# Eleven unread matrix products among the transposes of w2 and around the first scores

## The chip, the cores and the metric

The kernel runs on one core of a Trainium2 chip. The metric is the device time of one execution in microseconds. Of a kernel timed several times the median is given; one execution is profiled, and its span (first to last instruction) is a little shorter than its time.

## The reference

Four inputs q, k, v and f_logit have the shape batch 4, heads 8, sequence 768, head width 48. A gated linear recurrence runs over the sequence, and its output goes through a maxout layer.

```python
f = 1 / (1 + exp(-f_logit))
state = f[t][:, None] * state + outer(k[t], v[t])      # per batch and head, 48 x 48
y[t] = q[t] @ state
x = y as 3072 tokens x 384
out = maximum(x @ w1, x @ w2) @ w_out                   # w1, w2: 384 x 1024, w_out: 1024 x 384
```

## The kernel before

The sequence is cut into chunks of 128 positions; with four batches that makes 24 tiles, numbered i, each of all 8 heads. The first four tiles are the first chunks of the four batches, which have no earlier state.

For each tile, ACT computes exp and ln of the gate logits (`e`, `ln`), and TensorE sums the logs over the chunk with a triangular matrix (`cum`, L218). ACT turns the sums into factors `ei` and `ed`. DVE or GpSimd scales k and q with them (`kp`, `qp`, with `kpv`, `qpv` for those on DVE), TensorE transposes both (`trk`, `trq`, or `tr` for both at once, L263), and DVE copies the transposes out of PSUM (`trke`, `trqe`, `tre`). TensorE forms the scores of all heads (`a`, L281), DVE multiplies them with the causal mask (`am`, L286), and TensorE applies them to v (`y`, L326). ACT copies the result to `x`, TensorE transposes it (`xT`, L336).

The maxout is rewritten: max(h1, h2) is h2 plus the positive part of h1 - h2. So the kernel needs wd = w1 - w2 (`wd` on DVE, `wdp` on GpSimd) and w2o = w2 @ w_out. For w2o the prologue casts w2 to bf16 (`w2c` on DVE, `w2ca` on ACT), transposes it in eight blocks f of three 128 x 128 pieces (`w2T`, L186), copies each block out (`w2Te`, L189 on DVE), casts w_out (`woc`, L176 on ACT) and multiplies (`w2o`, L196). Each tile then takes x @ wd (`d0`, `d1`, L350), the positive part (`g0`, `g1`, on ACT) and x @ w2o + g @ w_out (`o0`, `o1`, L368), which DVE copies (`ob`) and a transfer stores.

The order of the instructions on every engine is written out by hand. The strings PROLOGUE, STEP and EPILOGUE list pairs of an operation's name and a number; `run` looks the name up in the table `ops` and issues it. Each engine, and SP's queue, which issues the loads, works through its own instructions in that order. PROLOGUE sets everything up to tile 6 or so, STEP repeats, EPILOGUE drains.

PSUM is divided into three pools: `ps_s` with three buffers (tag "s": cumulative sums, transposes, y, state products), `ps_a` with one buffer of two banks (tag "a": the scores), and `ps_m` with three buffers (tag "mm": transposed w2, w2o, d, o). The operation `warm n` takes one "mm" buffer and issues n products of 128 x 128 with 128 x 512 into it. Their inputs are the gate logs of tile 1, with zeros in the padding. Nothing reads their output; the buffer's next user overwrites it. The prologue has `warm 5`, `warm 3` and `warm 1`, nine products in all.

`run` drops an operation that was issued already, except `warm`.

Of the kernel before, what the change touches and what calls it, by code (L numbers as in the profile page):

```python
# [10 lines left out]
F32 = mybir.dt.float32  # L11
# [3 lines left out]


PROLOGUE = """
setup 0  setup 2  setup 1  lf 1  lf 0  lq 0  lw2 2  lk 0  lw2 0  lw2 1  lv 0  lwo 0  e 0
lwo 1  e 1  ln 1  lk 1  ln 0  cum 0  cum 1  lw1 0  w2ca 2  warm 5  ei 0  lw1 2  fl 0  ed 0
kp 0  ei 1  qpv 0  ed 1  fl 1  lw1 1  w2c 0  warm 3  warm 1  lq 1  w2ca 1  w2T 0  lf 2  w2T 7  # L20
trk 0  w2Te 7  trq 0  w2T 4  trke 0  w2Te 0  trqe 0  w2T 5  w2T 1  a 0  lv 1  am 0  w2Te 1
w2Te 4  v 0  lq 2  woc 2  w2T 2  y 0  w2Te 2  w2Te 5  woc 0  w2T 6  lk 2  w2T 3  woc 1  w2Te 6
w2o 2  kpv 1  w2o 1  x 0  w2Te 3  trk 1  lf 3  wdp 0  woc 3  xT 0  trke 1  w2o 5  xTe 0
w2o 4  w2o 7  w2o 10  lv 2  w2o 8  w2o 0  sa 0  wd 2  w2o 11  w2o 3  lk 3  w2oe 2  w2o 6
w2oe 1  w2o 9  wd 1  w2oe 0  lq 3  qpv 1  d1 0  lf 4  e 2  trq 1  d0 0  ln 2  trqe 1  tmp 0
lf 5  a 1  g0 0  v 1  cum 2  am 1  ed 2  lv 3  o0 0  g1 0  qp 2  ei 2  y 1  fl 2  lq 4  kpv 2
o1 0  x 1  xT 1  trk 2  xTe 1  lk 4  e 3  trq 2  trke 2  d0 1  ln 3  trqe 2  ob 0  lk 5
cum 3  a 2  v 2  ed 3  d1 1  g0 1  am 2  lv 4  ei 3  g1 1  o0 1  kpv 3  lq 5  y 2  qp 3
o1 1  x 2  fl 3  xT 2  lv 5  e 4  tr 3  xTe 2  ln 4  sa 1  d0 2  tre 3  lf 6  ob 1  cum 4
g0 2  a 3  d1 2  ed 4  lk 6  v 3  am 3  ei 4  g1 2  o0 2  lq 6  qp 4  e 5  tmp 1  y 3  fl 4  # L30
o1 2  x 3  st 0  lf 7  kpv 4  ln 5  xT 3  tr 4  xTe 3  sa 2  lk 7  cum 5  tre 4  d0 3  ob 2
a 4  lv 6  v 4  g0 3  d1 3  am 4  ei 5  ed 5  lv 7  g1 3  o0 3  qp 5  tmp 2  fl 5  y 4  kpv 5
lq 7  o1 3  x 4  st 2  xT 4  lq 9  e 6  tr 5  xTe 4  st 1  sa 3  ln 6  d0 4  tre 5  lf 8
ob 3  cum 6  g0 4  dq 4  a 5  v 5  d1 4  ed 6  am 5  lq 8  ei 6  qp 6  g1 4  o0 4  tmp 3  fl 6
out 2  e 7  y 5  kpv 6  o1 4  x 5  lk 8  ln 7  xT 5  tr 6  xTe 5  sa 4  lf 9  d0 5  tre 6
ob 4  cum 7  g0 5  dq 5  a 6  out 0  v 6  d1 5  ed 7  am 6  ei 7  lv 8  qp 7  g1 5  o0 5  tmp 4
y 6  kpv 7  out 1  o1 5  x 6  st 3  fl 7  xT 6  tr 7  lk 9  e 8  xTe 6  sa 5  ln 8  tre 7
lk 10  ob 5  v 7  lf 10
"""

STEP = """
# [23 lines left out]
def kernel(  # L65
# [13 lines left out]
    nc = tc.nc  # L79
    B, H, S, D = q.shape  # L80
    C = 128
# [6 lines left out]
    NP = H // 2  # L88
# [6 lines left out]
    ps_s = ctx.enter_context(tc.tile_pool(name="ps_s", bufs=3, space=bass.MemoryType.PSUM))  # L95
    ps_a = ctx.enter_context(tc.tile_pool(name="ps_a", bufs=1, space=bass.MemoryType.PSUM))
    ps_m = ctx.enter_context(tc.tile_pool(name="ps_m", bufs=3, space=bass.MemoryType.PSUM))
# [7 lines left out]
    ell_b = [consts.tile([C, H, DP], BF16, name=f"ell{n}") for n in range(2)]  # L105
# [10 lines left out]
    wd = consts.tile([C, JG, d_ff], BF16, name="wd")  # L116
    wo = consts.tile([C, FG, dm], BF16, name="wo")
    w2T = consts.tile([C, FG, dm], BF16, name="w2T")
    w2o = consts.tile([C, JG, dm], BF16, name="w2o")
# [23 lines left out]
    st = {}  # L143
# [209 lines left out]
    def a_g(i, half):  # L353
        s = st[i]
        if half == 0:
            s["g"] = work.tile([C, FG, C], BF16, name="gT", tag="gT", bufs=3)
        nc.scalar.activation(s["g"][:, half * 4:half * 4 + 4, :], psum.pop(("d", half, i)), AF.Relu)  # L357

    def p_o(i, half):
        s = st[i]  # L360
        if half == 0:
            psum["o", i] = ps_m.tile([C, dm], F32, name="o", tag="mm")
        mms = [(s["xT"][:, j, :], w2o[:, j, :]) for j in range(JG)]
        mms += [(lambda f=f: s["g"][:, f, :], wo[:, f, :]) for f in range(FG)]
        cut = 6
        for n in (range(0, cut) if half == 0 else range(cut, len(mms))):
            l, r = mms[n]
            nc.tensor.matmul(out=psum["o", i], lhsT=l() if callable(l) else l, rhs=r,  # L368
                             start=(n == 0), stop=(n == len(mms) - 1))
# [5 lines left out]
    def store(i, eng=nc.sync):  # L375
        c, b = divmod(i, B)
        r0 = b * S + c * C
        eng.dma_start(out=out[r0:r0 + C, :], in_=st[i]["ob"])
# [13 lines left out]
    def ob_last(h):  # L392
        t = st[T - 1]["ob", h] = consts.tile([C, dm // 2], F32, name=f"obl{h}")
        if h == 0:
            nc.scalar.copy(t, psum.pop(("last", h)))
        else:
            nc.vector.tensor_copy(t, psum.pop(("last", h)))
# [2 lines left out]
        r0 = B * S - C  # L400
        nc.sync.dma_start(out=out[r0:r0 + C, h * dm // 2:(h + 1) * dm // 2], in_=st[T - 1]["ob", h])

    def warm(n):

        ps = ps_m.tile([C, 512], F32, name="warm", tag="mm")
        for _ in range(n):
            nc.tensor.matmul(out=ps, lhsT=ell_b[1][:, 0:2, :].rearrange("p h d -> p (h d)"),
                             rhs=ell_b[1].rearrange("p h d -> p (h d)"), start=True, stop=True)

    ops = {  # L410
# [14 lines left out]
        "dq": lambda i: p_d(i, 1, True),  # L425
        "g0": lambda i: a_g(i, 0), "g1": lambda i: a_g(i, 1),
        "o0": lambda i: p_o(i, 0), "o1": lambda i: p_o(i, 1), "ob": v_ob, "out": store, "outa": lambda i: store(i, nc.scalar), "warm": warm,
        "lo": p_last, "lob0": lambda n: ob_last(0), "lob1": lambda n: ob_last(1),
        "lout": store_last,
    }  # L430
# [2 lines left out]
    done = set()  # L433

    def run(op, n):
        key = (same.get(op, op), n)
        if op == "warm" or key not in done:
            done.add(key)
            ops[op](n)

# [4 lines left out]
    for op, n in pairs(PROLOGUE):  # L445
        run(op, n)
    last = pairs(EPILOGUE)
    kept = split_up | {(same.get(op, op), n) for op, n in last}
    for i in range(FIRST_STEP, T + 8):
        for op, n in pairs(STEP):  # L450
            if 0 <= i + n < T and (same.get(op, op), i + n) not in kept:
                run(op, i + n)
    for op, n in last:
        run(op, n)
# [30 lines left out]
```

## Time and profile before

| what | value |
|---|---|
| time, median of 4 runs | 146.83 us (144.96 to 149.3) |
| time of the profiled execution | 144.96 us |
| its span | 143.2 us |
| mean granted TensorE clock | 0.988 |
| PE busy | 129.3 us, 90% of the span |
| PEld (weight loads) busy | 100.1 us, 70% |
| DVE busy | 106.5 us, 74% |
| ACT busy | 87.1 us, 61% |
| GpSimd (POOL) busy | 68.9 us, 48% |
| HBM traffic | 198 GB/s over the span |

In the profile, PE is TensorE's matrix products and PEld its weight loads, which overlap them; DVE is VectorE, ACT ScalarE, POOL GpSimd, and SP the engine that issues loads. A line such as L350 is a line of the kernel, and `out<-in` names the tiles written and read. The slices of the page cut the span into 40 equal parts; a digit is the busy share in tenths, and the clock row has the granted TensorE clock in tenths. The chain of waits is followed back from the last instruction to what released each step. Times stand in microseconds from the start of the span. An idle time before an instruction stands in brackets, with what ended it.

### The profile page before, as it was taken

What the parts mean: (1) busy time and instruction counts of PE and PEld (TensorE: products, weight loads), DVE (VectorE), ACT (ScalarE), POOL (GpSimd) and SP (SyncE); (2) the same over time, 40 slices, a digit from 0 to 9 for tenths busy, and PEclk for the clock granted to TensorE, in tenths of its full rate; (3) what the DMA queues carried; (4) which work ended last, traced back from release to release, by engine and by line L of the source; (5) the groups of instructions that cost most, each with busy time, mean ns of one, the idle gap of its engine ahead of it and who ended that gap; (6) DMA issues with size and microseconds to landing.
All of it is one profiled execution on the core that took longest, in us unless ns stands there. A gap on an engine that the chain in (4) does not pass through costs nothing.

```text
span 143.2 us, 4345 instructions
## 1 busy us (share of the span) xinstructions
PE 129.3 (90%) x1756; PEld 100.1 (70%) x1756; DVE 106.5 (74%) x191; ACT 87.1 (61%) x183; POOL 68.9 (48%) x98
## 2 busy tenths in 40 slices
PE   0096499999999999999999999999999999999981
PEld 0044357688778877887888788778878887887771
DVE  7825866796898789778977797798779777976521
ACT  3572454966677575758566765767585757663440
POOL 8520060220848485567657655855685546442000
PEclk9999959999999999999999999999999999999999
DMA  4999999999899997998999999999999999971111
GB/s 93 246 352 387 341 324 183 168 206 177 178 162 189 182 229 198 218 206 189 219 196 205 199 179 222 218 191 219 234 195 199 221 224 201 200 222 60 55 55 55
DMA packets 105764, 28.62 MB, mean 200 GB/s; under 512 B 101521, under 2 KB 104721, under 8 KB 105745
## 3 DMA queue, kind: packets, MB, share of 16 engines
q1 hardware_dynamic: 103728, 25.60, 85.6%
q10 hardware_dynamic: 2016, 2.75, 5.8%
q8 instruction: 13, 0.21, 0.6%
q14 instruction: 7, 0.05, 0.1%
HBM read 23.59 MB, written 4.72 MB: 198 GB/s over the span
## 4 chain that ended last, share of the span: by engine, by line
PE 85%; DMA 6%; SPq 5%; ACT 2%; issue 1%; DVE 1%
PE o L368 29%; PE d L350 25%; PE tr L263 7%; DMA wo_f<-in_moe_w_out_dram 6%; PE a L281 5%; PE w2op L196 4%; PE y L326 3%; PE xtp L336 3%; PE cum L218 3%; PE y L321 2%; PE sa L295 2%; SPq L152 2%; SPq L157 2%; SPq L161 1%; ACT wo L176 1%; PE o L389 1%
## 5 line engine op out<-in xcount | busy, mean ns | idle before, releaser
L350 PE MATMUL d<-xT,wd 128*128 128x128 bf16 x576 | 43.4, 220 | 0.5 <-DVE xT L340 0.4
L256 POOL TENSOR_TENSOR qp<-qt,ed 128x384 bf16<-128x384 f32 x22 | 22.1, 1003 | 44.4 <-ACT ed L230 30.5
L350 PEld LDWEIGHTS <-wd 128*128 128x128 bf16 x576 | 36.5, 114 | 4.3 <-issue 0.6
L368 PE MATMUL o<-wo,gT 128*128 128x384 bf16 x184 | 37.4, 325 | 0.0
L357 ACT ACTIVATE gT<-d 128x512 bf16<-128x512 f32 x48 | 28.9, 603 | 9.6 <-PE d L350 9.4
L286 DVE TENSOR_TENSOR am<-a,mask 128x1024 bf16<-128x1024 f32 x24 | 29.4, 1223 | 1.0 <-PE a L281 0.5
L340 DVE COPY xT<-xtp 128x384 bf16<-128x384 bf16 x24 | 8.6, 357 | 19.0 <-PE xtp L336 19.0
L368 PEld LDWEIGHTS <-gT 128*128 128x128 bf16 x184 | 16.2, 97 | 9.0
L310 POOL TENSOR_TENSOR st<-tmp,fl 64x192 bf16<-64x192 f32 x40 | 21.2, 529 | 2.7
L230 ACT ACTIVATE ed<-cum 128x384 f32<-128x384 f32 x24 | 11.8, 493 | 16.6 <-PE cum L218 15.5
L272 DVE COPY trs<-tr 128x1024 bf16<-128x1024 bf16 (+1 forms) x27 | 17.0, 631 | 4.6 <-PE tr L263 2.8
L331 ACT CAST x<-y 128x384 bf16<-128x384 f32 x24 | 11.5, 478 | 12.2 <-PE y L326 12.2
L237 POOL COPY flrow<-ed 32x384 f32<-32x384 f32 x16 | 17.8, 1113 | 1.0
L368 PE MATMUL o<-w2o,xT 128*128 128x384 bf16 x69 | 15.0, 326 | 0.0
L251 DVE TENSOR_TENSOR kp<-kt,ei 128x384 bf16<-128x384 f32 x23 | 14.3, 621 | 0.5 <-ACT ei L226 0.5
L218 PE MATMUL cum<-ell,ut 128*128 128x384 bf16 x24 | 8.1, 339 | 7.2 <-ACT ell L209 7.2
L205 ACT ACTIVATE e<-ft 128x384 f32<-128x384 f32 x24 | 12.5, 525 | 3.2 <-DMA ft<-in_f_logit_dram 3.2
L209 ACT ACTIVATE ell<-e 128x384 bf16<-128x384 f32 x24 | 12.5, 524 | 0.7
L373 DVE COPY ob<-o 128x384 f32<-128x384 f32 x23 | 12.6, 548 | 0.0
L226 ACT ACTIVATE ei<-cum 128x384 f32<-128x384 f32 x24 | 11.9, 497 | 0.0
L326 PE MATMUL y<-vb,am 128*128 128x48 bf16 x192 | 11.3, 184 | 0.2 <-DVE vb L213 0.2
L326 PEld LDWEIGHTS <-am 128*128 128x128 bf16 x192 | 9.7, 96 | 2.3 <-DVE am L286 0.4
(58 smaller groups left out, 171.9 us busy)
## 6 DMA issues: line engine op xcount, KB each, us to landing
ft<-in_f_logit_dram SPq DMA_DIRECT2D x24, 192.0 KB, 4.8
qt<-in_q_dram SPq DMA_DIRECT2D x24, 192.0 KB, 4.1
kt<-in_k_dram SPq DMA_DIRECT2D x24, 192.0 KB, 4.5
vt<-in_v_dram SPq DMA_DIRECT2D x24, 192.0 KB, 4.5
w_f<-in_moe_w_dram SPq DMA_DIRECT2D x6, 512.0 KB, 6.9
out_dram<-ob ACTq DMA_DIRECT2D x14, 192.0 KB, 3.4
out_dram<-ob SPq DMA_DIRECT2D x9, 192.0 KB, 3.3
wo_f<-in_moe_w_out_dram SPq DMA_DIRECT2D x2, 768.0 KB, 8.2
```

What stands on the lines that cost most here:

```text
L205: nc.scalar.activation(e, ld[i]["f"].rearrange("p h d -> p (h d)"), AF.Exp, scale=-1.0)
L237: nc.gpsimd.tensor_copy(row[:, :, 0:D, :].rearrange("s o d p -> s p o d"), st[i]["ed"][96:C, :].rearrange("s (p o d) -> s p o d", p=NP, o=2))
L251: eng.tensor_mul(s["kp"][:, :, 0:D], ld[i]["k"], s["ei"].rearrange("p (h d) -> p h d", h=H))
L256: eng.tensor_mul(s["qp"][:, :, 0:D], ld[i]["q"], s["ed"].rearrange("p (h d) -> p h d", h=H))
L272: nc.vector.tensor_copy(s["tr"][:, n:n + len(sel)], psum.pop(("tr" + sel, i)))
L286: nc.vector.tensor_mul(am.rearrange("p o n c -> p (o n) c"), psum.pop(("a", i)).rearrange("p o n c -> p (o n) c"), mask)
L310: nc.gpsimd.tensor_mul(st_b[b][(c + 1) % 2][r, :, e], st[i]["tmp"][r, :, e], st[i]["fl"][r, :].unsqueeze(2).to_broadcast([DP, NP, D]))
L326: nc.tensor.matmul(out=y[:, ds], lhsT=am[:, o, p, :], rhs=vb[:, ds], start=(c == 0), stop=(c == 0 or o == 1))
L350: nc.tensor.matmul(out=psum["d", half, i][:, n, :], lhsT=wd[:, j, ff(half * 4 + n)], rhs=st[i]["xT"][:, j, :], start=(j == 0), stop=(j == ...
L357: nc.scalar.activation(s["g"][:, half * 4:half * 4 + 4, :], psum.pop(("d", half, i)), AF.Relu)
L368: nc.tensor.matmul(out=psum["o", i], lhsT=l() if callable(l) else l, rhs=r, start=(n == 0), stop=(n == len(mms) - 1))
L373: nc.vector.tensor_copy(t, psum.pop(("o", i)))
```

## The change

Two operations are added to the table, and `warm` takes a pool, a tag and a shape. `warma n` issues n such products into the first bank of the scores' buffer of `ps_a`, and `warms n` issues n into a buffer of `ps_s`. PROLOGUE gets four of them, with everything else in its order: `warma 2` right after `warm 1`, ahead of the first transposes of w2; `warma 2` between `w2T 4` and `trke 0`; `warms 6` right after the first scores, `a 0`; and `warms 1` right after `y 0`. That is eleven products more. `run` lets every operation repeat whose name begins with "warm".

```diff
 PROLOGUE = """
 ...
-kp 0  ei 1  qpv 0  ed 1  fl 1  lw1 1  w2c 0  warm 3  warm 1  lq 1  w2ca 1  w2T 0  lf 2  w2T 7
-trk 0  w2Te 7  trq 0  w2T 4  trke 0  w2Te 0  trqe 0  w2T 5  w2T 1  a 0  lv 1  am 0  w2Te 1
-w2Te 4  v 0  lq 2  woc 2  w2T 2  y 0  w2Te 2  w2Te 5  woc 0  w2T 6  lk 2  w2T 3  woc 1  w2Te 6
+qpv 0  ed 1  fl 1  lw1 1  w2c 0  warm 3  warm 1  warma 2  lq 1  w2ca 1  w2T 0  lf 2  w2T 7
+trk 0  w2Te 7  trq 0  w2T 4  warma 2  trke 0  w2Te 0  trqe 0  w2T 5  w2T 1  a 0  warms 6  lv 1
+am 0  w2Te 1  w2Te 4  v 0  lq 2  woc 2  w2T 2  y 0  warms 1  w2Te 2  w2Te 5  woc 0  w2T 6  lk 2
 ...
-    def warm(n):
-
-        ps = ps_m.tile([C, 512], F32, name="warm", tag="mm")
+    def warm(n, pool=ps_m, tag="mm", shape=(C, 512)):
+        ps = pool.tile(list(shape), F32, name="warm", tag=tag)
         for _ in range(n):
-            nc.tensor.matmul(out=ps, lhsT=ell_b[1][:, 0:2, :].rearrange("p h d -> p (h d)"),
+            nc.tensor.matmul(out=ps.rearrange("p o n c -> p (o n c)")[:, 0:512] if len(shape) > 2 else ps,
+                             lhsT=ell_b[1][:, 0:2, :].rearrange("p h d -> p (h d)"),
                              rhs=ell_b[1].rearrange("p h d -> p (h d)"), start=True, stop=True)
 ...
+        "warms": lambda n: warm(n, ps_s, "s"), "warma": lambda n: warm(n, ps_a, "a", (C, 2, NP, C)),
 ...
-        if op == "warm" or key not in done:
+        if op.startswith("warm") or key not in done:
```

More of the change, by code (lines that the diff above doesn't have):

```diff
@@ L17 @@
 PROLOGUE = """
-setup 0  setup 2  setup 1  lf 1  lf 0  lq 0  lw2 2  lk 0  lw2 0  lw2 1  lv 0  lwo 0  e 0
-lwo 1  e 1  ln 1  lk 1  ln 0  cum 0  cum 1  lw1 0  w2ca 2  warm 5  ei 0  lw1 2  fl 0  ed 0
-kp 0  ei 1  qpv 0  ed 1  fl 1  lw1 1  w2c 0  warm 3  warm 1  lq 1  w2ca 1  w2T 0  lf 2  w2T 7
-trk 0  w2Te 7  trq 0  w2T 4  trke 0  w2Te 0  trqe 0  w2T 5  w2T 1  a 0  lv 1  am 0  w2Te 1
-w2Te 4  v 0  lq 2  woc 2  w2T 2  y 0  w2Te 2  w2Te 5  woc 0  w2T 6  lk 2  w2T 3  woc 1  w2Te 6
-w2o 2  kpv 1  w2o 1  x 0  w2Te 3  trk 1  lf 3  wdp 0  woc 3  xT 0  trke 1  w2o 5  xTe 0
@@ L24 @@
[L24 to L35, printed above, removed]
@@ L36 @@
-ob 4  cum 7  g0 5  dq 5  a 6  out 0  v 6  d1 5  ed 7  am 6  ei 7  lv 8  qp 7  g1 5  o0 5  tmp 4
-y 6  kpv 7  out 1  o1 5  x 6  st 3  fl 7  xT 6  tr 7  lk 9  e 8  xTe 6  sa 5  ln 8  tre 7
-lk 10  ob 5  v 7  lf 10
+setup 0  setup 2  setup 1  lf 1  lf 0  lq 0  lw2 2  lk 0  lw2 0  lw2 1  lv 0  lwo 0  e 0  lwo 1
+e 1  ln 1  lk 1  ln 0  cum 0  cum 1  lw1 0  w2ca 2  warm 5  ei 0  lw1 2  fl 0  ed 0  kp 0  ei 1
+qpv 0  ed 1  fl 1  lw1 1  w2c 0  warm 3  warm 1  warma 2  lq 1  w2ca 1  w2T 0  lf 2  w2T 7
+trk 0  w2Te 7  trq 0  w2T 4  warma 2  trke 0  w2Te 0  trqe 0  w2T 5  w2T 1  a 0  warms 6  lv 1
@@ new lines @@
+am 0  w2Te 1  w2Te 4  v 0  lq 2  woc 2  w2T 2  y 0  warms 1  w2Te 2  w2Te 5  woc 0  w2T 6  lk 2
+w2T 3  woc 1  w2Te 6  w2o 2  kpv 1  w2o 1  x 0  w2Te 3  trk 1  lf 3  wdp 0  woc 3  xT 0  trke 1
+w2o 5  xTe 0  w2o 4  w2o 7  w2o 10  lv 2  w2o 8  w2o 0  sa 0  wd 2  w2o 11  w2o 3  lk 3  w2oe 2
+w2o 6  w2oe 1  w2o 9  wd 1  w2oe 0  lq 3  qpv 1  d1 0  lf 4  e 2  trq 1  d0 0  ln 2  trqe 1
+tmp 0  lf 5  a 1  g0 0  v 1  cum 2  am 1  ed 2  lv 3  o0 0  g1 0  qp 2  ei 2  y 1  fl 2  lq 4
+kpv 2  o1 0  x 1  xT 1  trk 2  xTe 1  lk 4  e 3  trq 2  trke 2  d0 1  ln 3  trqe 2  ob 0  lk 5
@@ new lines @@
+cum 3  a 2  v 2  ed 3  d1 1  g0 1  am 2  lv 4  ei 3  g1 1  o0 1  kpv 3  lq 5  y 2  qp 3  o1 1
+x 2  fl 3  xT 2  lv 5  e 4  tr 3  xTe 2  ln 4  sa 1  d0 2  tre 3  lf 6  ob 1  cum 4  g0 2  a 3
+d1 2  ed 4  lk 6  v 3  am 3  ei 4  g1 2  o0 2  lq 6  qp 4  e 5  tmp 1  y 3  fl 4  o1 2  x 3
+st 0  lf 7  kpv 4  ln 5  xT 3  tr 4  xTe 3  sa 2  lk 7  cum 5  tre 4  d0 3  ob 2  a 4  lv 6  v 4
+g0 3  d1 3  am 4  ei 5  ed 5  lv 7  g1 3  o0 3  qp 5  tmp 2  fl 5  y 4  kpv 5  lq 7  o1 3  x 4
+st 2  xT 4  lq 9  e 6  tr 5  xTe 4  st 1  sa 3  ln 6  d0 4  tre 5  lf 8  ob 3  cum 6  g0 4  dq 4
@@ L39 @@
+a 5  v 5  d1 4  ed 6  am 5  lq 8  ei 6  qp 6  g1 4  o0 4  tmp 3  fl 6  out 2  e 7  y 5  kpv 6
+o1 4  x 5  lk 8  ln 7  xT 5  tr 6  xTe 5  sa 4  lf 9  d0 5  tre 6  ob 4  cum 7  g0 5  dq 5  a 6
+out 0  v 6  d1 5  ed 7  am 6  ei 7  lv 8  qp 7  g1 5  o0 5  tmp 4  y 6  kpv 7  out 1  o1 5  x 6
+st 3  fl 7  xT 6  tr 7  lk 9  e 8  xTe 6  sa 5  ln 8  tre 7  lk 10  ob 5  v 7  lf 10
 """
```

## The prediction

> **What bounds the kernel now.** First the slices of the page, since they show whether one engine is always busy and at which clock (40 slices of 3.58 us).
>
> ```profile
> PE   0096499999999999999999999999999999999981
> PEclk9999959999999999999999999999999999999999
> DMA  4999999999899997998999999999999999971111
> ```
>
> From the sixth slice on PE is full, so whatever delays PE there delays the end. One slice, 17.9 to 21.5 us, ran at half the clock. The DMA engines are as full as PE, which matters below. Second, the chain that ended last, at the place where PE takes it over:
>
> ```profile
> 7.97 8.34 DMA wo_f<-in_moe_w_out_dram
> 16.34 1.58 ACT wo L176 x2
> 17.96 1.44 PE w2op L196 x4
> 19.40 0.43 PE tr L263 x4
> 19.83 0.32 PE xtp L336 x3
> 20.15 2.49 PE w2op L196 x12
> ```
>
> Until 17.96 us the end hangs on the second w_out transfer and two casts; PE before that is off the chain. From 17.96 on it is PE, nearly without a break. Third, the order of PE's work before that point, with its idle time:
>
> ```profile
> 14.11 0.33 PE L186 MATMUL w2tp<-ident,w_h 128*128 128x128 bf16 x3 [0.26 <-DVE w2T L189]
> 14.44 0.40 PE L281 MATMUL a<-trs 48*128 48x128 bf16 x8
> 16.42 0.36 PE L186 MATMUL w2tp<-ident,w_h 128*128 128x128 bf16 x3 [1.58 <-DVE w2T L189]
> 16.95 0.36 PE L326 MATMUL y<-vb,am 128*128 128x48 bf16 x8 [0.17 <-DVE vb L213]
> 17.15 0.51 PE L186 MATMUL w2tp<-ident,w_h 128*128 128x128 bf16 x6
> ```
>
> PE idles 1.58 us behind the mask product of DVE, and little around it. Fourth, busy time and clock in stretches of 3.41 us, cut where the clock changes:
>
> ```profile
> 10.88:14.29 3.41, 2.33 (x26) 1.53 (x24) 1.94 (x6) 1.04 (x1) 0.00 (x0) 1.00 1.03 386
> 14.29:17.70 3.41, 1.61 (x28) 1.17 (x26) 2.83 (x8) 1.36 (x2) 0.00 (x0) 1.00 1.08 339
> 17.70:21.11 3.41, 3.15 (x15) 1.88 (x15) 2.16 (x6) 2.05 (x4) 2.35 (x1) 0.50 1.11 341
> ```
>
> The second number is PE's busy time, the last but two the clock. A stretch with 1.61 us of matmul is followed by one at half clock; one with 2.33 us is not. Last, the products of the kind that is added:
>
> ```profile
> L407 PE MATMUL warm<-ell x9: 379/634/634, 8.0 to 11.2; 128*128 128x512 bf16 x9
> ```
>
> They start 0.427 us apart until 10.88 us, then about 0.22 apart: the slow clock and the full one.
>
> [...]half pace until 10.88, half from 17.70 to 21.11 (3.41 us), then full to the end.[...]
>
> **The change part by part.** Eleven products of 512 columns are added, 2, 2, 6 and 1. At full clock 11 x 0.213 = 2.35 us of PE, at half clock 11 x 0.427 = 4.70 us. Nothing is removed or moved; no load, store, ACT, DVE or POOL instruction changes, and SP's and POOL's queues are passed by nothing.
>
> Two before the first w2 transposes: the last product of warm-up now runs from 11.15; two more fill PE to about 11.79. The first transpose of w2 moves from 11.69 to 11.79, the next waits for ACT's cast until 12.60 anyway. Cost 0.
>
> Two after the third transposed block: from 13.52 to 13.95 instead of the next six transposes, of which three waited until 14.11 and now go out by about 14.29. The scores wait for DVE's copy until 14.44. Cost 0, with 0.15 us to spare; at half clock the 0.85 us would push the scores some 0.4 us.
>
> Six after the scores: 14.66 to 15.94, inside the idle 1.58 us that ends at 16.42. Cost 0; at half clock 2.56 us, ending at 17.2, pushing w2T, y and what follows.
>
> One after y 0: from 17.15, so the two transposed blocks behind it end issue at 17.71 in place of 17.50. The w2o product waits for ACT until 17.96. DVE's copy of the first block moves about 0.2 us, and with it the k product of tile 1, from 18.35 to some 18.57. Cost 0 on PE.
>
> PSUM: the first four products take the scores' bank before any score exists, the other seven a buffer of the "s" pool. Of its users before, the last copy ends at 14.38, ahead of 14.66. Two extra turns of three buffers shift the rotation, but each later user then still follows the same kind of predecessor; price 0, at most the drain of a product, 0.17 us (379 ns less the 213 of its stream). The product's inputs are read long before ln of tile 3 rewrites them at 28.7 us.
>
> What it gives: the stretch 14.29 to 17.70 goes from 1.61 to about 1.61 + 7 x 0.213 = 3.10 us busy, above the 2.33 that kept the clock. Then 17.70 to 21.11 runs at full clock. Rebuilt from there: four w2o matmuls 4 x 0.1625 = 0.65 us, to 18.61; the transposes of k (needing DVE at 18.57) to 18.87; the x transposes wait for ACT's x, which ends at 19.02 behind three casts, so PE stands 0.2 us, to 19.25; twelve w2o matmuls, 1.95, to 21.20; sa 0.17; eight more, 1.30, to 22.67. Before, this point was 24.11. So PE is **1.44 us** ahead, not the whole 1.7 of the half-clock stretch. DVE, which waited 1.25 us for PE at 18.6, has wd done at about 22.4 in place of 23.18, in time.
>
> What is late next: the loads. SP waits for nothing of the compute between 1 and 44 us; its issues last about 1 us each, as long as one 192 KB load takes to land after the other. So these landings don't move when PE does. Landing of a load against the start of its user, plus the spare time to PE: k of tile 2 lands 26.88, used 27.78, transposed 0.15 after it could be: 1.05 us in all. f of tile 3, 27.73 to 28.17 plus 0.54: 0.98. f of tile 6, 42.16 to 42.66 plus 0.55: 1.05. The tightest is k of tile 4, issued 31.09, 5.5 us to land, 36.58: DVE multiplies from 37.10 to 38.10, PE transposes at 38.16. Spare to PE: none, so **0.52 us**. Of the 1.44, about 0.5 is left behind tile 4, and PE, full thereafter, carries it to the end. Bounds: 0 if the loads land slightly later, 1.44 if they land sooner.
>
> The sum: profiled execution 144.96 (span 143.2 and 1.76 around it), less 0.5: 144.4. The median of the four runs is 146.83, 1.87 above, and they spread from 144.96 to 149.3. No view tells why. [...]leave a quarter of the 1.87: 144.4 + 0.5 = **144.9**.
>
> **The rivals.** The likeliest case: clock held, gain capped by loads, spread mostly gone: 144.9 (143.8 to 146.0), chance 0.50.
>
> Loads follow[...]: the full 1.44 us and no spread, 144.96 - 1.44 = 143.5 (143.0 to 143.9), 0.22. For it: landings have jitter (two arrived 2 us apart from 34.60 to 36.58), so the 0.52 may be chance. Against: DMA is at 1.0 in every stretch to 50 us.
>
> The spread isn't the clock's: only the 0.5 shows, 146.83 - 0.5 = 146.3 (145.9 to 147.0), 0.13. This also covers the products failing to hold the clock (0 gained, 146.8), for which little speaks, 3.10 being well over 2.33.
>
> Slower: the products meet a slow clock. If [...]the clock is half at 14.4, the six last 2.56 us where 1.8 is free, and the one 0.43; y and the last transposes end about 19.0, so w2o starts 1.05 us late: 147.9. It decides once the clock is half from 14.4 to 17.7. With the first four in the way as well, 4.70 us less some 1.8 of gaps: 2.9, to 149.7. For it: the first release came at 10.88[...]. 0.15.
>
> **How the numbers follow.** Two per cent, about what a measurement of this kernel can tell from no change, is 143.9 and 149.8. Faster: the second case and 0.06 of the first, 0.28. Slower: 0.06 of the last. Same: 0.66. The range, 143.4 to 147.2, leaves out the low end of the second case and most of the last, 0.2 together.
>
> **What would show it.** The clock row has no half slice after the first release; w2o matmuls at 326 ns and not 524; the idle time before w2T at 16.4 shrinks to some 0.3 with its start unmoved; the first d product starts near 22.7 in place of 24.11; then new small waits, DVE's k product or ACT's exp on their loads, near 27, 28 and 37 us, which eat the lead to about 0.5. Wrong would be: a half slice elsewhere, w2o starting after 18.0, no load waits (then the gain is 1.4), or the spread of the timed runs unchanged.

## The result

The changed kernel has a median of 145.95 us (144.66 to 148.95, 43 runs) beside 146.54 us for the kernel before (144.89 to 149.97, 64 runs). The ratio is 0.9985 with an interval of 0.9963 to 1.0007: no difference that can be measured. The ratios and their intervals leave out slow executions, those over 1.5% above the fastest of their kernel, and the medians don't, so a ratio can't be read off two medians. The forecast of 144.9 lay 1.1 us too low.

The profile after is of an execution of 145.44 us (span 143.7, mean clock 0.996). Its slices, for PE and its clock:

```profile
PE   0099999999999999999999999999999999999981
PEclk9999999999999999999999999999999999999998
```

The half-clock slice is gone, as forecast; the last digit is after PE's work. PE's timeline at the added products (line numbers moved by one or two):

```profile
7.92 4.85 PE L405 MATMUL warm<-ell 128*128 128x512 bf16 x11
...
13.66 0.59 PE L405 MATMUL warm<-ell 128*128 128x512 bf16 x2
14.09 0.50 PE L185 MATMUL w2tp<-ident,w_h 128*128 128x128 bf16 x6
14.59 0.40 PE L280 MATMUL a<-trs 48*128 48x128 bf16 x8
14.92 1.47 PE L405 MATMUL warm<-ell 128*128 128x512 bf16 x6
16.57 0.36 PE L185 MATMUL w2tp<-ident,w_h 128*128 128x128 bf16 x3 [0.19 <-DVE w2T L188]
17.10 0.36 PE L325 MATMUL y<-vb,am 128*128 128x48 bf16 x8 [0.17 <-DVE vb L212]
17.30 0.38 PE L405 MATMUL warm<-ell 128*128 128x512 bf16 x1
```

Here the clock first went to full (its first release, below) at 12.79 us, where it was 10.88 before, so the first eleven products ran at half clock: they start 0.43 us apart, the six behind the scores 0.22. The scores still start at 14.59 (14.44 before); the transfer of w2 for which ACT's cast waits landed 0.15 us later in this execution. The six products lie in the old gap, and y follows 0.15 us after its old time. In the same execution w2o starts at 18.10 (17.96 before), still behind ACT's cast, whose w_out transfer landed 0.13 us later, and its twelve matmuls take 2.11 us in place of 2.69. Cut from 12.79 us on in pieces of 3.41 us, as long as the half-clock stretch of the kernel before, the stretches (columns as before) are:

```profile
12.79:16.20 3.41, 3.41 (x39) 2.15 (x38) 2.46 (x6) 0.00 (x0) 0.00 (x0) 1.00 1.08 358
16.20:19.61 3.41, 2.92 (x32) 1.79 (x32) 2.89 (x11) 3.14 (x5) 0.87 (x1) 1.00 1.02 392
```

So the products do what they were to do. One limit of the clock record has to be known: it begins with the first release, and what lies before counts as full clock (1.00 in the kernel before from 7.47 to 10.88 us, where products start 0.427 us apart). The mean clock of an execution therefore doesn't tell when the first release came. In thirteen of the fourteen profiles here it came between 9.85 and 12.79 us, and in one at 16.11.

Where did the lead go? Set against the kernel before, the transposes of k, one set a tile, are a ruler: tile 2 starts at 27.98 (28.58 before, 0.60 us ahead), tile 3 at 32.78 (33.38, 0.60), tile 4 at 37.98 (38.16, 0.18), tile 7 at 52.69 (52.86, 0.17), tile 8 at 57.89 (57.76, 0.13 *behind*), tile 20 at 116.69 (116.56), tile 21 at 121.96 (121.46, 0.50 behind). There are three steps, and each has its line. The first d product waits for wd:

```profile
23.37 0.81 PE L349 MATMUL d<-xT,wd 128*128 128x128 bf16 x11 [0.34 <-DVE wd L178]
```

At tile 4 PE waits for DVE's product of k:

```profile
37.98 0.40 PE L262 MATMUL tr<-ident,kp 128*128 128x128 bf16 x4 [0.28 <-DVE kp L250]
```

The load of k landed at 36.83, where it had been 36.58, but the product began 0.5 us later still. GpSimd was copying a row of gate factors (`flrow`) meanwhile. The two, before and then after:

```profile
36.98 0.89 POOL L237 COPY flrow<-ed 32x384 f32<-32x384 f32 x1
37.10 1.00 DVE L251 TENSOR_TENSOR kp<-kt,ei 128x384 bf16<-128x384 f32 x1
```

```profile
36.72 0.88 POOL L236 COPY flrow<-ed 32x384 f32<-32x384 f32 x1
37.36 0.56 DVE L250 TENSOR_TENSOR kp<-kt,ei 128x384 bf16<-128x384 f32 x1 [0.61 <-ACT x L330]
```

(The bracket names ACT's copy of y because it ended last; before, the product started without it.) The product takes 0.55 us where GpSimd doesn't overlap it (17.80 us before, 18.16 after). In eight of the fourteen profiles the copy began first; the product then ends 0.23 or 0.24 us after the copy, in this one 0.32. In the other six the product began first; it takes 0.55 or 0.56 us, and the copy takes 1.27 to 1.29 in place of 0.88. Here the delay stands ahead of the product's record and not in it, from k's landing to 37.36 us, but the end fits the same pattern. So I read the copy as what set this step, with k's landing adding some 0.1 us (an estimate, 0.32 less 0.23). The copy stands behind GpSimd's product of q, whose load landed at 35.49, 34.60 before. That product started only 0.27 us ahead of its old time.

And tile 8's gate logits, which ACT needs, landed at 53.13 (51.65 before). From ACT's timeline:

```profile
53.15 0.53 ACT L204 ACTIVATE e<-ft 128x384 f32<-128x384 f32 x1 [0.77 <-DMA ft<-in_f_logit_dram]
```

The step at tile 21 is of another kind. The chain of waits there, in order of time:

```profile
115.38 5.46 DMA vt<-in_v_dram
120.84 0.02 issue
120.86 0.34 ACTq L377
121.20 0.04 issue
121.24 0.49 ACT x L330
121.73 0.05 issue
121.78 0.34 PE xtp L335 x3
```

L377 is an output store, issued on ACT's queue. It waited for the landing of a load of v, although it stores something else, and ACT's copy of y stood behind it. In the trace the store waits for semaphore 110, and the load of v, issued at 115.38 us, names 110 too. The load landed at 120.84 us, with the last rise of 110 before the store, and the store went out at 120.86. No forecast of mine had this wait.

### The profile page after: what moved, and what is told of

Its sections match the earlier page's. It is cut to its first block, busy times and chain, and to the rows that moved or that the text cites. A ratio compares the mean times of both kernels' runs of the same rounds, so it can differ in the third digit from the quotient of the medians.

```text
span 143.7 us, 4367 instructions
## 1 busy us (share of the span) xinstructions
PE 131.6 (92%) x1767; PEld 100.3 (70%) x1767; DVE 106.7 (74%) x191; ACT 87.5 (61%) x183; POOL 69.4 (48%) x98
## 4 chain that ended last, share of the span: by engine, by line
PE 54%; SPq 32%; DMA 7%; issue 2%; ACT 2%; DVE 1%; ACTq 0%; DVEq 0%
SPq L151 25%; PE o L367 19%; PE d L349 17%; SPq L156 5%; PE tr L262 5%; DMA vt<-in_v_dram 4%; PE a L280 4%; DMA ft<-in_f_logit_dram 4%; PE y L325 2%; PE xtp L335 2%; PE y L320 2%; PE cum L217 2%; PE sa L294 2%; SPq L160 1%; PE o L388 1%
## 5 line engine op out<-in xcount | busy, mean ns | idle before, releaser
L250 DVE TENSOR_TENSOR kp<-kt,ei 128x384 bf16<-128x384 f32 x23 | 13.7, 595 | 1.1 <-ACT x L330 0.6
```

What stands on the lines that cost most here:

```text
L250: eng.tensor_mul(s["kp"][:, :, 0:D], ld[i]["k"], s["ei"].rearrange("p (h d) -> p h d", h=H))
```

## The experiments

Theory 1 is that loads bind the start and absorb PE's lead. Its rivals: the products cost what they save; PE alone sets the end; the clock makes the spread of the times. Theory 4 (wd holds the first d products) and theory 5 (stores on ACT's queue hold PE late in the kernel) came with the readings above.

The runs were timed in three groups, each beside the kernel before. Its median was 146.18 us in the first (light loads, twelve products, sorted loads), 145.51 in the second (the wd step, the store moved on ACT) and 145.64 in the third (stores on GpSimd, parts of the change). So times compare within a group; across groups only the ratios do. Intervals of differences are of the medians of the executions on record.

### Light loads, without and with the products

Eleven loads, v of tiles 2 to 12, are left out of each kernel, and k is read in their place, so the output is another.

```diff
         for name in names:
+            if name == "v" and 2 <= i <= 12:
+                ld[i]["v"] = ld[i]["k"]
+                continue
             t = loads.tile([C, H, D], F32, name=f"{name}t", tag=f"{name}t")
```

> The kernel before, with the v loads of tiles 2 to 12 left out: these tiles take their k in place of v, so 11 of the transfers of 192 KB before 80 us are gone (some 11 us of transfer time) and all else is as it was; the output is not the reference's. Theory 1 (loads bound the start: from 20 to 62 us what lands late sets PE's start, and so the spread of the times too): faster than the kernel before by some 1 us at the median (the transfers' lateness goes), at most 1.5, and a narrower spread, near 144.9 to 145.5. Theory 2 (PE alone bounds, loads have nothing to do with it): no change, 146.5. Theory 3[...]: spread as wide as before.

> The changed kernel with the same 11 v loads left out (k in place of v in tiles 2 to 12; the output is not the reference's). Theory 1: with the loads out of the way PE keeps its lead, 0.6 us as read at tile 2 in the profile after to 1.44 as worked out; so it stands 0.6 to 1.4 us under the other kernel with light loads, near 144.0. Theory 2 (the products cost as much as they save, so that there is no lead to lose): equal to the other kernel with light loads, within 0.3 us.

Measured: without the products 145.0 us (144.24 to 147.53, 22 runs), ratio to the kernel before 0.9944 [0.9916, 0.9972]; with them 144.53 us (144.15 to 145.52, 16 runs), 0.9922 [0.9895, 0.995]. So loads do bound the start and do make spread: half of the executions lie within 0.5 us without the products and 0.6 with them, within 1.7 for the kernel before. With the loads out of the way the products gain 0.46 us in the medians (interval 0.1 to 0.7), 0.3 by the ratios. That is short of the 0.6 to 1.4 expected, so loads were not the only absorber.

The clock record of each execution gives a second comparison inside one kernel. Some executions have a half-clock stretch after the first release (mean clock 0.988 or less; 3.41 us of the 143.2 in the profile before) and others don't (0.995 or more; the end of the span takes up to 0.005, in the profile after 0.004, at half clock from 142.50 us on). Light loads without products: 145.05 us with the stretch (15 executions), 144.53 without (7), the latter the time with products (difference between -0.1 and +0.8). Of the kernel before itself, measured beside all experiments, 114 executions with the stretch have a median of 145.79 us and 44 without 145.70 (difference between -0.6 and +0.6; one execution of 715.75 us is left out). **With all loads in place no cost of the half-clock stretch can be seen at the median; with light loads it looks like 0.5 us.** The intervals are too wide to tell these two from each other by the clock record alone.

### Six more products

```diff
-... a 0  warms 6  lv 1
+... a 0  warms 12  lv 1
```

> The changed kernel with 12 in place of 6 products after the first scores: 6 x 0.213 = 1.28 us more on PE at 16.4 us, where 0.2 us is idle, so w2o starts about 1 us later. Theory 1 (loads bind until 62 us): most of it is hidden as the lead was, below +0.5 us against the changed kernel, so between 145.9 and 146.5. Theory 2 (PE alone sets the end): +1.0 us, 147.0.

Measured: 146.63 us (144.84 to 149.01, 14 runs), ratio to the kernel before 0.9997 [0.995, 1.0044]. In its profile the last of the twelve ends at 17.5 us, w2o starts at 18.41 where ACT's cast would allow 17.95, and the first d products still wait for DVE, to 23.63. The profiled execution took 145.02 us all the same. But 5 of the 14 executions had a half-clock stretch, and these took 147.5 to 149.0 us; the other nine have a median of 146.0. So in the profile a w2o that starts 0.46 us late hides behind wd and the loads. The rival of products met by a slow clock isn't shown by the five: their record has only the mean clock, not where the stretch lay. In the kernel before, half clock followed a stretch with PE busy for 1.61 of 3.41 us, and a PE that stands still for a late load has a sparse stretch too; so the half-clock stretch may be the effect of the lateness and not its cause.

### Sorted loads

The loads of tiles 2 to 10 keep their 33 places in the prologue, but stand in the order of their use.

```diff
-lf 2 lq 2 lk 2 lf 3 lv 2 lk 3 lq 3 lf 4 lf 5 lv 3 lq 4 lk 4 lk 5 lv 4 lq 5 lv 5 lf 6 lk 6 ...
+lf 2 lq 2 lk 2 lf 3 lq 3 lv 2 lk 3 lf 4 lq 4 lv 3 lf 5 lk 4 lv 4 lq 5 lk 5 lf 6 lv 5 lq 6 ...
```

> The changed kernel with the loads of tiles 2 to 10 in the prologue put in the order in which the profile before uses them, at the same places of the order (those of f for tiles 8 and 10, of k for tile 4 and others move ahead; those of q for tile 9, k for tiles 5 and 10, f for tile 5 move back). Theory 1: what bound was the tight loads, f of tiles 6, 8, 10 and k of tile 4, with others landing 3 to 7 us early; sorted, the lead stays for the most part: 0.5 to 1.0 us faster than the changed kernel, near 145.1. Theory 2: no change, 146.0. A third: only the sum of bytes counts, order nothing: no change.

Measured: 146.32 us (144.3 to 148.31, 22 runs), ratio to the kernel before 0.9962 [0.9926, 0.9999]. The median was missed, but the ruler shows the point: tile 4 at 37.46 (38.16 before), tile 8 at 57.07 (57.76), tile 18 at 106.07 (106.76). The lead of 0.7 us now lives through the loads. It is lost later, in two waits of PE for ACT's copy of y at 116.0 and 121.5 us, where PE idles 0.18 and 0.40 us and the ruler loses 0.35 and 0.58, both behind an output store that waited for a load of v. Three executions had a half-clock stretch, at 147.4 to 148.3, though this kernel has all eleven products; where it lay isn't on record.

### The wd step

GpSimd subtracts the first third of wd, DVE the others. GpSimd's line and DVE's lines, before and then after:

```profile
18.61 2.35 POOL L179 TENSOR_TENSOR wd<-w_f 128x1024 bf16<-128x1024 f32 x1 [7.99 <-DMA w_f<-in_moe_w_dram]
```

```profile
20.47 2.71 DVE L179 TENSOR_TENSOR wd<-w_f 128x1024 bf16<-128x1024 f32 x2
```

```profile
18.74 2.35 POOL L178 TENSOR_TENSOR wd<-w_f 128x1024 bf16<-128x1024 f32 x1 [8.40 <-DMA w_f<-in_moe_w_dram]
```

```profile
20.04 3.27 DVE L178 TENSOR_TENSOR wd<-w_f 128x1024 bf16<-128x1024 f32 x2
```

DVE starts 0.43 us earlier and ends 0.13 us later. GpSimd's line too moved 0.13 us, with the landing of w1. In all eleven profiles in which the two overlap, DVE's first subtraction ends 1.07 to 1.09 us after GpSimd's. In the next two kernels GpSimd's part is left out, together with the eleven loads.

```diff
-w2o 2  kpv 1  w2o 1  x 0  w2Te 3  trk 1  lf 3  wdp 0  woc 3 ...
+w2o 2  kpv 1  w2o 1  x 0  w2Te 3  trk 1  lf 3  woc 3 ...
-            ... lhsT=wd[:, j, ff(half * 4 + n)],
+            ... lhsT=wd[:, max(j, 1), ff(half * 4 + n)],
```

> The changed kernel with light loads (v of tiles 2 to 12 left out, k in its place) and also without GpSimd's subtraction for the first row block of wd; the d products read the second block in its place, so the output is not the reference's. Theory 4 (the step between w2o and d is set by wd: DVE's first subtraction ends 1.08 us after GpSimd's, in all profiles, so d can't start before 23.1 to 23.5 us whatever PE does): wd is then ready by about 22.5, the 0.5 us of idle PE before the first d goes, and the time falls by 0.4 to 0.6 us against the light kernel with GpSimd's subtraction, to some 144.0. Its rival (wd late for another reason, such as w1's landing at 21.2 us): no change, 144.5.

> The kernel before with the same two parts left out (v of tiles 2 to 12, GpSimd's subtraction; the output is not the reference's). Here both absorbers of the lead are gone. If theory 1 and 4 together hold, the half-clock stretch now costs its worked-out price: the executions whose clock has it are 0.9 to 1.4 us slower than those without and than the changed kernel in this form, near 145.0; those without it are near 144.0. If only the loads mattered: 0.5 us, as with light loads alone. If neither: none.

Measured: with the products 143.96 us (143.82 to 144.35, 6 runs), ratio 0.9905 [0.9876, 0.9933]; without them 144.28 us (143.78 to 145.13, 8 runs), 0.9926 [0.9895, 0.9957]. Against light loads with GpSimd's part the ratio fell from 0.9922 to 0.9905, about 0.25 us with overlapping intervals (the times, 144.53 and 143.96, are of two groups and don't compare). So theory 4's 0.4 to 0.6 us isn't shown by the times. That GpSimd's part holds wd is shown by the lines. DVE's and PE's with the products:

```profile
19.84 2.57 DVE L181 TENSOR_TENSOR wd<-w_f 128x1024 bf16<-128x1024 f32 x2
```

```profile
22.60 0.83 PE L352 MATMUL d<-xT,wd 128*128 128x128 bf16 x12
...
26.29 0.37 PE L328 MATMUL y<-vb,am 128*128 128x48 bf16 x8 [0.28 <-DVE am L288]
```

The first twelve d products now go without a break, at 22.60, close to the 22.67 of the forecast. Without products, the executions with the half-clock stretch have 144.65 us (4), those without 143.94 (4). The stretch now seems to cost 0.71 us (0.1 to 1.2), less than the 0.9 to 1.4 expected. In the profile with products some of the lead goes at y of tile 1, whose mask product waits behind the cast of v of tile 1, a load that these kernels still have; it landed at 24.71 and was cast from 24.74.

### The late stores

In the repeated step the store is moved behind ACT's ln of the next tile. The loads are sorted too, with products and without.

```diff
-... lq 3  g1 -1  outa -4
+... lq 3  g1 -1
-... tr 1  ln 2  xTe 0  sa -1
+... tr 1  ln 2  outa -4  xTe 0  sa -1
```

> The changed kernel with the loads of tiles 2 to 10 sorted by their use, and in the repeated step the output store on ACT's queue moved from ahead of the copy of y to behind the ln of the next tile, where ACT is idle for about 1 us. Theory 5 (late in the kernel the store waits on ACT for the landing of a load of v, and holds the copy of y, which holds PE by 0.3 to 0.6 us each time; this, not the clock, makes most of the spread): the spread narrows, and the lead won at the start reaches the end: 0.5 to 1.0 us below the sorted kernel, median near 145.0. Rival (PE is late there for the landings themselves): as the sorted kernel, 146.

> The kernel before with the same two moves (loads sorted, store moved), without the products. Theory 1: with the loads sorted the start no longer absorbs all of the lead, so this one is 0.3 to 0.6 us slower than the same with the products (wd keeps the rest), and faster than the kernel before by about 0.5 to 1.0 at the median. If the products bring nothing in any order: equal to it within 0.2.

Measured: with products 145.17 us (144.18 to 147.62, 22 runs), ratio 0.9962 [0.9935, 0.9988]; without 145.7 us (144.37 to 149.16, 22 runs), 0.9999 [0.9972, 1.0026]. By the ratio, 0.9962 as with sorted loads alone, moving the store gained nothing, and it did not end the waits: in the profile with products PE still idles 0.16 and 0.29 us at 109.8 and 115.2 us. The store now waits for loads of q and k, and ACT's exp stands behind it. The ratios with and without products differ by 0.4%, with intervals that overlap. The profile without products happened to catch an execution in which the first release came only at 16.11 us, after stretches with 2.55 and 2.57 of 3.41 us busy at half pace, and two half-clock stretches followed, 19.5 to 26.3 us: the first d product at 27.89 us, 4 us late, span 147.1. Executions with more than one half-clock stretch, a mean clock under 0.98, are 12 of 158 of the kernel before and none of 132 of all the kernels with the eleven products or more.

So the store was taken off ACT altogether and given to GpSimd's queue.

```diff
-        ... "outa": lambda i: store(i, nc.scalar), ...
+        ... "outa": lambda i: store(i, nc.gpsimd), ...
-... qp 1  fl 1  ei 1  lq 3  g1 -1  outa -4
+... qp 1  fl 1  outa -4  ei 1  lq 3  g1 -1
```

> The changed kernel with the loads sorted as before and the output stores of the repeated step issued from GpSimd's queue in place of ACT's, behind its product of q. Theory 5 (a store on ACT's queue waits for the landing of some load and holds the copy of y, wherever it stands in ACT's order): with the wait on GpSimd, which idles some 2 us each step, the late stalls of PE (0.3 to 0.6 us each, near 110 to 122 us) go; median near 144.7, spread within 1 us for most, ratio to the kernel before about 0.990. Rival (the landings themselves hold PE, or GpSimd's issue of stores costs it what ACT saves): 145.2 or more, no better than with the store moved on ACT.

> The kernel before with the same two moves as the last one (loads sorted, stores from GpSimd's queue), without the products. If the lead of the products now reaches the end: 0.4 to 0.7 us slower than the same with the products (what wd leaves of the lead), and with some executions at 148 or more where the clock has several half stretches. If the lead is lost elsewhere still: equal within 0.2.

Measured: with products 144.6 us (144.32 to 145.8, 8 runs), ratio 0.9946 [0.9916, 0.9977]; without 145.2 us (144.46 to 148.91, 22 runs), 0.9972 [0.9952, 0.9992]. Both have no late wait of PE behind ACT left in their profiles, and the spread shrank: half of the executions without products lie between 145.07 and 145.49, where half of the kernel before in the same group lie between 145.19 and 146.03. GpSimd issues the store in 0.58 us:

```profile
115.63 0.58 POOL L379 DMA_DIRECT2D out_dram<-ob  x1
```

It goes out as GpSimd's updates of the state end (114.35 us, 1.33 long), and ACT's copy of y, at 115.18 us in the same profile, waits for y alone (0.56 us). Whether the store would have to wait for a load on GpSimd's queue too isn't shown: the move may change two things at once, the engine that issues and what the store waits for.

And now the products are worth **0.4 to 0.6 us**: 0.6 by the medians (145.2 to 144.6, interval 0.5 to 0.9, though of only 8 executions with products), 0.4 by the ratios. The ruler agrees with the smaller: 0.40 us ahead at tile 2 (27.97 against 28.37) and still 0.40 at the last tile (130.65 against 131.05). That this is the price of the half-clock stretch isn't shown by the clock record: without products 17 executions with the stretch have 145.18 us and 5 without 145.24 (145.70 and 145.56 with the store moved on ACT, 16 and 6). The version with products, sorted loads and stores on GpSimd lies half a per cent below the kernel before. The changed kernel wasn't timed in the same group; its own ratio was 0.9985.

### Parts of the change

```diff
-... warm 3  warm 1  warma 2  lq 1 ...      -... w2T 4  warma 2  trke 0 ...
+... warm 3  warm 1  lq 1 ...               +... w2T 4  trke 0 ...
```

> The changed kernel with only the seven products around the first scores (6 and 1), without the four among the transposes. By the stretches of the profile[...] these seven are what keeps the clock between the scores and w2o: executions with a clock under 0.995 fall from about three in four to few[...]. The time: as both kernels, 145.9, since the lead is absorbed.

```diff
-... a 0  warms 6  lv 1 ...      -... y 0  warms 1  w2Te 2 ...
+... a 0  lv 1 ...               +... y 0  w2Te 2 ...
```

> The changed kernel with only the four products among the transposes of w2 (2 and 2), without the seven around the first scores. The idle 1.58 us behind the scores stays, so the half-clock stretch should stay in about three of four executions as in the kernel before; the rare executions with several half stretches (8 in 102 of the kernel before, median 149.1) should go if these four help the first release to hold. The time: 145.9 to 146.2.

Measured: the seven around the scores alone 145.78 us (144.83 to 149.16, 14 runs), ratio 1.0002 [0.9972, 1.0031], 3 of 14 executions with a clock under 0.995 (one of them at 0.994, less than a whole stretch); the four among the transposes alone 145.55 us (144.64 to 149.51, 22 runs), 1.0008 [0.9981, 1.0035], 11 of 22 (three in four were expected). The kernel before has it in 114 of 158, the changed kernel in none of 44. So the seven do most, and the four seem to cover the rest; neither moves the time. Each part alone still had one execution over 149 us, with a clock of 0.975 and 0.962, so the four alone don't end the rare ones, which had been expected of them.

## Why the prediction was right or wrong

**What bounds before 17.96 us, and that the products hide there: right.** Scores, y and w2o kept their times within 0.15 us, which later transfers explain, though the first eleven products ran at half clock. In this profile every cost put at nothing held; no wait for a PSUM buffer shows.

**The clock is held: right for the changed kernel.** After the first release it is full in all 44 executions with a clock record, against 44 of 158 of the kernel before. In the variants it isn't always: 3 of 22 with sorted loads and 5 of 14 with twelve products lost it somewhere.

**The lead of 1.44 us: the first step that failed.** "DVE has wd done at about 22.4 in place of 23.18, in time" was wrong: it ended at 23.31, and d waited. I moved DVE's subtractions with their start and left out GpSimd's at the same time. In the traces the end of DVE's first subtraction moved with GpSimd's, 1.08 us behind it before and after: it took 1.57 us with 0.49 us of GpSimd's beside it and 2.14 with 1.06, where the second took 1.21 with none. And without GpSimd's part (and with light loads) the d products started at 22.60. The lead was 0.60 us at tile 2.

**The tightest load: right in place, by luck.** At tile 4 the lead did fall, to 0.18 us, but k's landing was not the main cause. The reading took 36.58 to 37.10 us as k's spare time and the product's 1.00 us as its length; alone it takes 0.55, and the rest was GpSimd's copy, as at wd. Some 0.33 us of the lead went with q's landing, through GpSimd's product and that copy, and some 0.1 with k's, as read from this one profile. The step that followed, "PE, full thereafter, carries it to the end", failed too: the landings vary by more than the lead that is left, and f of tile 8, 1.5 us later than before, took the remainder. Sorted loads, with q of tile 4 landing at 32.63, carried 0.7 us to 106 us, which fits that the loads' order, and not PE, held it back.

**The 1.87 us from the profiled execution to the median: the step that failed by most.** The forecast put most of this spread down to the clock, an estimate that no view had shown. Most of it isn't the clock's: no difference shows in the kernel before between executions with and without the half-clock stretch, and the changed kernel, whose clock stays full after the first release in every execution, still goes from 144.66 to 148.95. A late first release, which the mean clock doesn't tell, is the rival that is left. It is unlikely to make most of that range: the light kernel with products, open to the same releases, stays within 144.15 to 145.52 in 16 executions. The forecast kept a quarter of the 1.87. From the fastest execution to the median it is 1.65 us before and 1.29 after, so four fifths stay. The 1.87 itself came from four executions of which the profiled one was the fastest. Only a small part is the clock's: 4 of 158 executions of the kernel before had a mean clock near 0.95 and took 149.3 to 151.3 us. Late loads make much of the rest: light loads cut it (half of the executions within 0.5 us in place of 1.7), and so did sorted loads with stores on GpSimd's queue (0.42 in place of 0.84).

**The rival that won** is the one given 0.13, that the spread isn't the clock's. Its 0.5 us lies at the edge of what was measured, 0.2 us by the ratio, between -0.1 and 0.5. The rival of a late w2o did not show in the changed kernel; whether the late executions with sorted loads and with twelve products are of its kind is open.

That the store ahead of tile 21's transposes waits for a load of v is read from the trace of the profile after, where both name semaphore 110. No run changes the semaphore and leaves the store on ACT's queue. Nor was a faster wd tried in a kernel with all loads, or a tile 4 without GpSimd's copy.

## What to carry to other kernels

A lead on the bounding engine is worth what its *next* suppliers allow: before counting it, list for each coming step the landing of its load and the work of other engines beside which its producer ran longer in the trace (here DVE's product of k, 1.00 us beside GpSimd's copy and 0.55 alone), and take the smallest spare time. Where times spread, compare executions by the suspected cause (here each one's clock record) before putting the spread down to it. Here a store issued from ACT's queue held ACT's compute by 0.6 us; look for such a transfer in the chain of waits wherever the ruler of equal steps jumps.

## What had not been expected of the hardware

DVE's subtraction for wd, 1.21 us alone, took 2.14 when it began 1.06 us before GpSimd's of the same kind ended. DVE's product of k, 0.55 us alone, took 1.00 at tile 4 of the kernel before, when GpSimd's copy had begun 0.12 us earlier; begun 0.16 us before the copy, as at 80.60 us there, it took 0.55, and the copy 1.14 in place of 0.88. At tile 4 the one of the two that began first was not delayed, in all fourteen profiles; at tile 6, before and after, the copy began 0.02 us first and still took 1.31 us, the product 0.54. A stretch of 3.41 us with PE busy for 1.61 and a longest idle time of 1.58 was followed by half clock, and so was one with 1.66 busy (store moved on ACT, no products), while full clock followed 1.83 (light loads, no products) and 2.92 (the profile after). Every stretch here that half clock followed holds a gap of 1.58 us or more, and none that full clock followed holds one over 1.12, as a stretch's end cuts the gap in the light run. So it isn't shown whether the busy share counts, with which the prediction reckons, or the longest gap. Output stores on ACT's queue, 0.34 us each, held ACT until an unrelated load had landed, 0.6 us after its own previous work was done (120.25 to 120.86 us in the profile after); with the stores on GpSimd's queue no late wait of PE behind ACT is left in the profiles.
